# Where neighbouring blocks are paired in an S4 convolution: input spectra paired in DRAM by adding transfers, or kernel spectra paired by VectorE

## The chip, the cores and the metric

The kernel runs on one core of one Trainium2 chip. The metric is the device time of one execution in microseconds (us). The time before is the median of three runs.

## What is computed

Two layers, each of them an S4 convolution and a SwiGLU feed-forward, each on a normalised input and added to the stream `x` (2048 rows of 512):

```python
x = x + conv(layernorm(x));  x = x + ffn(layernorm(x))      # twice
# conv: K[d,l] = Re(sum_n C*exp(dt*A*l)*dt*B), y = causal convolution of u with K over 2048 rows, + u * Dskip
# ffn:  (silu(x @ w_gate) * (x @ w_up)) @ w_down,  w: 512 x 1376 and 1376 x 512
```

Both layers use the same convolution kernel `K` and the same weights.

## The kernel before

The convolution is done by blocks. The 2048 rows are four blocks of 512 rows (`NB = 4`). Each block of the input and of `K` is turned into a spectrum of odd frequencies (four groups `q` of 128 frequencies, two halves `h` of 256 columns, real and imaginary part: one tile of 128 x 512 f32, 256 KB). A block of the output, at these frequencies, is a sum of products of input spectra with kernel spectra; the part of a product that runs over a block's end belongs to the next block, with its real and imaginary part swapped and one of them negated. Before, this pairing of neighbours is put into the kernel spectra: what is stored as the spectrum of lag block k is that of block k plus the turned one of block k-1.

**Spectra of K (until some 345 us).** `K` is built in eight chunks of 64 columns. For each, VectorE and ScalarE make powers (`gen_e` L433-L440, `gen_g` L447-L475, `gen_turns`, `gen_trig`, `gen_exp`), TensorE multiplies them (`lags`, L485 and L486), the result goes through DRAM into the layout `kt` (`spread`, L498 and L500), and `spectra` multiplies it with DFT matrices (L515, products of 128x256 f32), two calls a chunk, each for two groups `q`. In `spectra` ScalarE copies the swapped and signed spectrum of block k-1 (L542) and the spectrum of lag block 0 (`w0r`, L543), VectorE adds the spectrum of block k (L545), and SP stores the sum to DRAM (`wdr`). For the last two chunks `first_parts` and `later_parts` (L576-L578) do this. The direct term `Dskip` is added inside the products by a matmul of one row (L517, L560). Beside this run the spectra of input blocks 0 and 1 of layer 0 (`direct`, L289-L293, stored by SP to `udr`), and the sizes of the FFN weights (`norms`, with the reduction L329 on VectorE).

The order of the three compute engines and of SP is written out by hand here: a list of (time, step) entries, sorted by time (`prepare`, `factors`, `use`, `second_block`, `weights`), with chunk starts 28 to 31 units apart. An engine takes its instructions in that order.

**The blocks (345 us on).** The order is `SEQ`: (layer, block) = (0,0), (0,1), (0,2), (1,0), (0,3), (1,1), (1,2), (1,3). While TensorE does the FFN of one entry (L886-L903), the convolution of the next entry goes on beside it. For each half and group: `forward` makes z on VectorE (L229), splits it for f16 (ScalarE L263, VectorE), TensorE multiplies (L273), ScalarE copies the spectrum `u` out (L275), and POOL stores it to `udr` for later blocks (L706, blocks 0 to 2 only). Then VectorE multiplies each input spectrum with its kernel spectrum (L754, 128x1024) and sums the products (L757): first lag block 0, `u` from SBUF with `w0r`, then k = 1 to b with `w` and `uu` that SP loads (L750, L752). L758 and L759 finish `y`, and TensorE (L773) and VectorE turn it back. Generators run one step ahead (`ahead`); beyond that the order of the engines in this part is set at build time by a scheduler with its own estimate of durations.

Of the kernel before, what the change touches and what calls it, by code (L numbers as in the profile page):

```python
# [11 lines left out]
F32 = mybir.dt.float32  # L12
# [10 lines left out]
P = 128  # L23
# [5 lines left out]
NL = 2  # L29
# [44 lines left out]
def kernel(ctx, tc, x, a_re, a_im, b_re, b_im, c_re, c_im, log_dt, d_skip,  # L74
# [65 lines left out]
    one = sb.tile([P, 1], F32, name="one")  # L140
    G.memset(one, 1.0)
# [4 lines left out]
    udr = [dram.tile([NB - 1, 2, 4, P, 2, HD], F32, name=f"udr{i}") for i in range(NL)]  # L146
# [95 lines left out]
    def forward(n, h, eh):  # L242
# [13 lines left out]
        for i, q in enumerate(QORD):  # L256
# [9 lines left out]
            with tc.high_priority(offset=BOOST):  # L266
# [8 lines left out]
                A.activation(u, pf, AF.Copy, scale=2.0 ** -16 if eh else 1.0)  # L275
            yield q, u
# [6 lines left out]
    def direct(b, h, q, n, space=psml):  # L283
# [9 lines left out]
        nc.sync.dma_start(udr[0][b, h, q], u)  # L293
# [194 lines left out]

    def spread_in(pk):
        ks = tl([P, 4, 16, 16], "ks", "nn")  # L490
        A.activation(ks, pk.rearrange("p d (c a) -> p a c d", a=4), AF.Copy)
        return ks
# [18 lines left out]
    def products(ch, pw, kt, k0, k1, q, order):  # L511

        for i, c in order:
            e = ek[q // 2][:, q % 2, c - 1, i] if c else ef[:, q, i]
            PE.matmul(pw[:, i], lhsT=e, rhs=kt[:, :, c + 4 * k0:4 * k1:4, :].rearrange("p g k d -> p k g d"), start=c == 0, stop=c == 3)  # L515
            if (i, c) == (0, 0) and k0 == 0:
                PE.matmul(pw[:, 0, 0], lhsT=one[0:1].to_broadcast([1, P]), rhs=dsk[:, ch * DC:(ch + 1) * DC], start=False, stop=False)  # L517

    def signs(q):

        return enumerate((-1.0, 1.0) if q % 2 == 0 else (1.0, -1.0))
# [4 lines left out]
    def spectra(ch, kt, q0):  # L526
# [4 lines left out]
        for j in range(2):  # L531
            products(ch, pw[:, j], kt, 0, NB, q0 + 2 * j, [(i, c) for i in range(2) for c in range(4)])
# [8 lines left out]
        for i, sign in signs(q0):  # L541
            A.activation(wv[:, :, i], pv[:, :, 1 - i, :3 * DC], AF.Copy, scale=sign)  # L542
        A.activation(w0r[:, h, q0::2, :, off:off + DC], wf[:, :, :, 0], AF.Copy)  # L543
        yield
        V.tensor_tensor(wv, pv[:, :, :, DC:], wv, OP.add)  # L545
# [5 lines left out]
    def first_parts(c0, q):  # L551
# [3 lines left out]
        for c in range(4):  # L555
            for i in range(2):
                e = ek[q // 2][:, q % 2, c - 1, i] if c else ef[:, q, i]
                PE.matmul(pw[:, i], lhsT=e, rhs=kt2[:, c0 + 2 - NCH:, :, c], start=c == 0, stop=c == 3)
                if (i, c) == (0, 0):
                    PE.matmul(pw[:, 0], lhsT=one[0:1].to_broadcast([1, P]), rhs=dsk[:, c0 * DC:], start=False, stop=False)  # L560
        A.activation(w0r[:, 1, q, :, off:], pw.rearrange("p i k g d -> p i (k g d)"), AF.Copy)

    def later_parts(ch, kt, qs=QORD):
# [3 lines left out]
        for q in qs:  # L567
            pw = psml([P, 2, NB - 1, 4, 16], "pw")
            products(ch, pw, kt, 1, NB, q, [(0, c) for c in range(4)])
            yield  # L570
            products(ch, pw, kt, 1, NB, q, [(1, c) for c in range(4)])
            yield
            w0 = w0r[:, h, q, :, off:off + DC].rearrange("p i (g d) -> p i g d", g=4)
            wo = next(slots)
            for i, sign in signs(q):
                A.activation(wo[:, i, 0], w0[:, 1 - i], AF.Copy, scale=sign)  # L576
                A.activation(wo[:, i, 1:], pw[:, 1 - i, :2], AF.Copy, scale=sign)
            V.tensor_tensor(wo, pw, wo, OP.add)  # L578
# [657 lines left out]
```

## Time and profile before

| | |
|---|---|
| runs (us) | 1185.04, 1185.14, 1187.83; median 1185.14 |
| profiled execution | 1186.51, its span 1184.7 |
| mean granted TensorE clock | 0.991 |
| TensorE busy | 1117.3 us (94%) |
| VectorE busy | 1006.2 us (85%) |
| ScalarE busy | 587.1 us (50%) |
| POOL busy | 92.2 us (8%) |
| DMA | 151.17 MB, 128 GB/s |

The page's rows carry the line of the kernel, the engine, the operation, out<-in, the shapes and the count; then the busy time and the mean duration of one in ns; then the idle time of the engine just before these instructions and what ended it. A row of a wait table is: engine, tile and line that waited, what was waited for, the time in all, how often, and the longest. A window row gives the busy time of each engine in a stretch of the span.

### The profile page before, as it was taken

The page shows a single profiled execution, that of the slowest core. Times are in us where ns is not written, and L with a number is a line of the kernel's source. Part 1 is how long each engine was busy: PE and PEld are TensorE (multiplying, and loading weights), DVE is VectorE, ACT ScalarE, POOL GpSimd, SP SyncE. Part 2 cuts the span into 40 slices and gives each one's busy share as a digit, 9 for nine tenths or more (in the row PEclk, how much of TensorE's full clock was granted, in tenths as well). Part 3 has the DMA queues.
Part 4 walks back from the last instruction along what each step waited for, and adds up shares of the span by engine and source line. Part 5 has one row for each costly group of instructions (what it writes and reads, how often), then busy time and mean ns, then how long its engine had stood idle before and what let it go on. Part 6 is the DMA issues. An engine that isn't in the chain of part 4 may idle for free.

```text
span 1184.7 us, 24523 instructions
## 1 busy us (share of the span) xinstructions
PE 1117.3 (94%) x10008; PEld 884.8 (75%) x10008; DVE 1006.2 (85%) x1591; ACT 587.1 (50%) x1180; POOL 92.2 (8%) x151
## 2 busy tenths in 40 slices
PE   1979999999789988999999999989999999999998
PEld 1868888888776857777778687858777686876875
DVE  7999999987789898999899999989994899983211
ACT  6677888833461554546654443655533452324211
POOL 1011111110000010002000000211000010000000
PEclk9989999999899999999999999999999999999999
DMA  6266666757484337432353354333544144312000
GB/s 231 91 162 149 162 166 162 182 179 240 125 271 140 115 119 200 118 96 84 92 152 128 112 165 155 96 104 115 149 116 165 46 121 130 118 49 45 14 24 18
DMA packets 136532, 151.17 MB, mean 128 GB/s; under 512 B 75474, under 2 KB 83666, under 8 KB 136419
## 3 DMA queue, kind: packets, MB, share of 16 engines
q1 hardware_dynamic: 129314, 126.47, 35.8%
q0 software_dynamic: 7104, 23.14, 7.3%
q8 instruction: 78, 1.28, 0.5%
q14 instruction: 36, 0.29, 0.1%
HBM read 101.85 MB, written 31.46 MB: 113 GB/s over the span
## 4 chain that ended last, share of the span: by engine, by line
PE 37%; DVE 27%; issue 4%; DMA 4%; ACT 2%; SPq 1%; POOL 0%; DVEq 0%; ACTq 0%; POOLq 0%
PE pgu L886 6%; PE pgu L887 6%; PE pgu L889 6%; DVE t L754 5%; DVE yk L757 5%; PE py L901 4%; PE py L902 3%; PE py L903 3%; PE pi L773 3%; PE pf L273 3%; DVE yk L754 2%; DVE z L229 2%; DVE sg L893 2%; DMA mix<-nn 1%; DVE bb L229 1%
## 5 line engine op out<-in xcount | busy, mean ns | idle before, releaser
L886 PE MATMUL pgu<-mix,wsl 128*128 128x256 f16 x1280 | 299.7, 273 | 6.9 <-DVE sg L893 4.4
L887 PE MATMUL pgu<-mix,wsl 128*128 128x256 f16 x1280 | 299.7, 273 | 0.0
L889 PE MATMUL pgu<-mix,wsl 128*128 128x256 f16 x1280 | 195.6, 273 | 0.0
L887 PEld LDWEIGHTS <-wsl 128*128 128x128 f16 x1280 | 125.5, 98 | 24.3 <-issue 8.0
L901 PE MATMUL py<-wsl,hh 128*128 128x512 f16 (+1 forms) x352 | 134.2, 381 | 8.6 <-DVE xg L906 6.9
L886 PEld LDWEIGHTS <-wsl 128*128 128x128 f16 x1280 | 125.4, 98 | 16.0
L889 PEld LDWEIGHTS <-wsl 128*128 128x128 f16 x1280 | 125.5, 98 | 14.9
L903 PE MATMUL py<-wsl,hl 128*128 128x512 f16 (+1 forms) x352 | 134.1, 381 | 0.2 <-DVE hl L895 0.2
L902 PE MATMUL py<-wsl,hh 128*128 128x512 f16 x320 | 121.8, 381 | 0.0
L754 DVE TENSOR_TENSOR t<-uu,w 128x1024 f32<-128x1024 f32 x96 | 116.9, 1218 | 2.6 <-DMA w<-wdr 2.4
L757 DVE TENSOR_TENSOR yk<-yk,t 128x1024 f32<-128x1024 f32 x96 | 116.9, 1217 | 0.3
L892 ACT ACTIVATE sg<-pgu,sc 128x512 f32<-128x512 f32 x80 | 54.6, 683 | 121.0 <-PE pgu L889 115.9
L893 DVE SCALAR_TENSOR_TENSOR sg<-pgu,sc,sg 128x512 f32<-128x512 f32 x80 | 59.6, 745 | 56.6 <-ACT sg L892 56.5
L515 PE MATMUL pw<-kt,ek 128*128 128x256 f32 (+1 forms) x384 | 94.1, 382 | 0.0
L894 ACT ACTIVATE hh<-sg 128x512 f16<-128x512 f32 x80 | 50.0, 626 | 76.1 <-DVE sg L893 76.0
L773 PE MATMUL pi<-yl,mix 128*128 128x256 f16 x576 | 78.9, 273 | 5.0 <-DVE yl L229 2.7
L515 PEld LDWEIGHTS pw<-kt,ek 128*128 128x128 f32 x384 | 70.8, 194 | 8.9
L273 PE MATMUL pf<-z,eh 128*128 128x256 f16 x576 | 74.9, 273 | 0.0
L754 DVE TENSOR_TENSOR yk<-u,w0r 128x1024 f32<-128x1024 f32 x56 | 68.2, 1218 | 1.5 <-ACT u L275 1.5
L902 PEld LDWEIGHTS <-hh 128*128 128x128 f16 (+1 forms) x352 | 34.6, 98 | 46.1 <-issue 10.6
L895 DVE TENSOR_TENSOR hl<-sg,hh 128x512 f16<-128x512 f32 x80 | 54.8, 686 | 15.6 <-ACT hh L894 15.5
L485 PE MATMUL pk<-re,g 128*32 128x64 f32 x1024 | 65.0, 317 | 2.8 <-DVE re L440 2.8
(239 smaller groups left out, 2154.3 us busy)
## 6 DMA issues: line engine op xcount, KB each, us to landing
w<-wdr SPq DMA_DIRECT2D x96, 256.0 KB, 2.7
uu<-udr SPq DMA_DIRECT2D x96, 256.0 KB, 3.0
udr<-u POOLq DMA_DIRECT2D x32, 256.0 KB, 2.7
g<-acc POOLq DMA_DIRECT2D x6, 1024.0 KB, 8.4
udr<-u SPq DMA_DIRECT2D x16, 256.0 KB, 2.1
n<-ndr SPq DMA_DIRECT2D x16, 256.0 KB, 3.9
n<-xdr SPq DMA_DIRECT2D x4, 1024.0 KB, 5.7
kdr<-ks SPq DMA_DIRECT2D x6, 512.0 KB, 2.7
```

The source lines that it names most:

```text
L273: PE.matmul(pf[:, o], lhsT=e, rhs=m, start=k == 0, stop=k == len(terms) - 1)
L515: PE.matmul(pw[:, i], lhsT=e, rhs=kt[:, :, c + 4 * k0:4 * k1:4, :].rearrange("p g k d -> p k g d"), start=c == 0, stop=c == 3)
L754: V.tensor_tensor(t, uu.unsqueeze(1).to_broadcast([P, 2, 2, HD]), w.unsqueeze(2).to_broadcast([P, 2, 2, HD]), OP.mult)
L757: V.tensor_tensor(yk, yk, t, OP.add)
L773: PE.matmul(pi[:, o], lhsT=e, rhs=m, start=k == 0, stop=k == len(terms) - 1)
L886: PE.matmul(o, lhsT=wgu(wi, k, 0)[:, fs], rhs=nh[:, k], start=k == 0, stop=False)
L887: PE.matmul(o, lhsT=wgu(wi, k, 1)[:, fs], rhs=nh[:, k], start=False, stop=False)
L889: PE.matmul(o, lhsT=wgu(wi, k, 0)[:, fs], rhs=nlo[:, k], start=False, stop=k == 3)
L893: V.scalar_tensor_tensor(sg, pgu[:, 1], sc6[:, 4:5], sg, OP.mult, OP.mult)
L901: PE.matmul(py[:, r], lhsT=hh[:n, f, rc], rhs=wd(f, 0)[:n], start=f == 0, stop=False)
L902: PE.matmul(py[:, r], lhsT=hh[:n, f, rc], rhs=wd(f, 1)[:n], start=False, stop=False)
L903: PE.matmul(py[:, r], lhsT=hl[:n, f, rc], rhs=wd(f, 0)[:n], start=False, stop=f == FT - 1)
```

## The change

- `udr` now holds **paired** input spectra: U_b plus the swapped, signed U_(b-1). For blocks 0 to 2, a new function `carry` makes a negated copy of one half of `u` on ScalarE (128x256) and issues two transfers of 128 KB to the next block's slot in `udr`, the halves swapped: from SP for the spectra made in the first part, from ScalarE's queue in `forward`. Then, for blocks 1 to 3, POOL stores `u` with an **adding transfer** into that slot (`accum_op=OP.add`). Block 3 has a slot now.
- The kernel spectra stay unpaired: L542's two copies, L545, L576, L577's two and L578 become one ScalarE copy.
- In the convolution, for b > 0, the spectrum for lag block 0 is loaded from `udr` too, so each step loads one `uu` more, and k runs from b down to 0.
- The direct term is added to lag 0 of `kt` by VectorE (`skip`, 64 elements in one partition, one call a chunk), in place of the one-row matmuls.
- In the list: the call of `skip` at t + 17.1, no fourth entry for `spectra`, the last part of `gen_e` in four entries, and two later times for the reductions of `weights`.

```diff
-    udr = [dram.tile([NB - 1, 2, 4, P, 2, HD], F32, name=f"udr{i}") for i in range(NL)]
+    udr = [dram.tile([NB, 2, 4, P, 2, HD], F32, name=f"udr{i}") for i in range(NL)]
...
 # forward
+            G.dma_start(udr[layer][b, h, q], u, **(dict(accum_op=OP.add) if b else {}))
+            if b < NB - 1:
+                carry(udr[layer][b + 1, h, q], q, u, nc.scalar)
             yield q, u
...
 # direct
-        nc.sync.dma_start(udr[0][b, h, q], u)
+        if b:
+            G.dma_start(udr[0][b, h, q], u, accum_op=OP.add)
+        else:
+            nc.sync.dma_start(udr[0][b, h, q], u)
+        carry(udr[0][b + 1, h, q], q, u, nc.sync)
...
+    def skip(ch, kt):
+        k = kt[0:1, :, 0]
+        V.tensor_tensor(k, k, dsk[:, ch * DC:(ch + 1) * DC].rearrange("p (g d) -> p g d", g=4), OP.add)
...
 # products
-            if (i, c) == (0, 0) and k0 == 0:
-                PE.matmul(pw[:, 0, 0], lhsT=one[0:1].to_broadcast([1, P]), rhs=dsk[:, ch * DC:(ch + 1) * DC], start=False, stop=False)
...
+    def carry(o, q, u, eng):
+        n = 1 - q % 2
+        t = tl([P, HD], "neg", "t1")
+        A.activation(t, u[:, n], AF.Copy, scale=-1.0)
+        eng.dma_start(o[:, 1 - n], t)
+        eng.dma_start(o[:, n], u[:, 1 - n])
...
 # spectra
-        for i, sign in signs(q0):
-            A.activation(wv[:, :, i], pv[:, :, 1 - i, :3 * DC], AF.Copy, scale=sign)
+        A.activation(wv, pv[:, :, :, DC:], AF.Copy)
         A.activation(w0r[:, h, q0::2, :, off:off + DC], wf[:, :, :, 0], AF.Copy)
-        yield
-        V.tensor_tensor(wv, pv[:, :, :, DC:], wv, OP.add)
...
 # later_parts
-            for i, sign in signs(q):
-                A.activation(wo[:, i, 0], w0[:, 1 - i], AF.Copy, scale=sign)
-                A.activation(wo[:, i, 1:], pw[:, 1 - i, :2], AF.Copy, scale=sign)
-            V.tensor_tensor(wo, pw, wo, OP.add)
+            A.activation(wo, pw, AF.Copy)
...
 # ssm_half
-            for k in range(b + 1):
-                if k == 0:
-                    w, uu = w0r[:, h, q], u
-                else:
+            for k in range(b, -1, -1):
+                w, uu = w0r[:, h, q], u
+                if k:
                     w = tl([P, 2, HD], "w", "w")
                     nc.sync.dma_start(w, wdr[k, h, q])
+                if b:
                     uu = tl([P, 2, HD], "uu", "uu")
                     nc.sync.dma_start(uu, udr[layer][b - k, h, q])
...
 # the list
-            at(t + 22.0, ge, 100)
+            for k in range(4):
+                at(t + 22.0 + 0.6 * k, ge, 1 if k < 3 else 100)
...
+            at(t + 17.1, lambda: skip(c, kt))
...
-            for k, t0, t1, t2, t3 in ((0, -1.4, 8.0, 13.9, 17.0), (1, 8.1, 14.5, 17.45, 19.5),
+            for k, t0, t1, t2, t3 in ((0, -1.4, 8.0, 13.9, 22.3), (1, 8.1, 14.5, 17.45, 22.9),
```

Lines of the changed kernel differ by a few from those of before. Two places show what moves on **VectorE**. The first is one chunk in the first part, from the last of `gen_turns` (`im<-im`) to the first rows of the next chunk's `gen_g`; `re` and `im` are the powers, `cmx` the reduction for the weight sizes, `spare` and `wo` the paired kernel spectra. Before:

```order
L386 ISA im<-im 128x2048
L329 TENSOR_REDUCE cmx<-nrm 128x1
L545 TENSOR_TENSOR spare<-pw,spare 128x768
L435 TENSOR_TENSOR re<-re 128x2048
L437 SCALAR_TENSOR_TENSOR im<-im,mu 128x1984
L440 TENSOR_TENSOR re<-re,mu 128x124x8 x2
L447 TENSOR_TENSOR xz<-xz,mz_158 128x960
L451 TENSOR_TENSOR g<-w_154,re 128x2x64
L452 TENSOR_TENSOR spare<-w_154,im 128x2x64
L433 TENSOR_TENSOR im<-im,re 128x2048
L545 TENSOR_TENSOR wo<-pw,wo 128x768
```

The same place of the changed kernel, where `kt_470<-kt_470,tdk` is `skip`:

```order
L391 ISA im<-im 128x2048
L497 TENSOR_TENSOR kt_470<-kt_470,tdk 1x4x16
L440 TENSOR_TENSOR re<-re 128x2048
L334 TENSOR_REDUCE cmx<-nrm 128x1
L442 SCALAR_TENSOR_TENSOR im<-im,mu 128x1984
L445 TENSOR_TENSOR re<-re,mu 128x124x8 x2
L452 TENSOR_TENSOR xz<-xz,mz_156 128x960
L456 TENSOR_TENSOR g<-w_152,re 128x2x64
L457 TENSOR_TENSOR spare<-w_152,im 128x2x64
L438 TENSOR_TENSOR im<-im,re 128x2048
```

Both additions of 768 elements are gone, `skip` stands where the first of them and the reduction stood, and the reduction follows one long instruction later.

The second place is the start of block (1,2) on VectorE. `z<-z` is the last step of the first group's spectrum on VectorE, before TensorE's L273; the product with `w0r` is the first that needs this spectrum. Before:

```order
L229 SCALAR_TENSOR_TENSOR z_3112<-z_3112 128x2x256
L229 SCALAR_TENSOR_TENSOR z_3112<-bt 128x256 x2
L229 SCALAR_TENSOR_TENSOR bb<-pi,sy,bb 128x512
L754 TENSOR_TENSOR yk<-u,w0r 128x1024
L229 SCALAR_TENSOR_TENSOR z_3112<-z_3112 128x2x256
```

In the changed kernel four more rows stand between `z<-z` and the first of these (an `sg`, two of `z<-bt`, an `hl`), and the product with `w0r` is the last:

```order
L227 SCALAR_TENSOR_TENSOR bb<-pi,sy,bb 128x512
L227 SCALAR_TENSOR_TENSOR z_3100<-z_3100 128x2x256
L227 SCALAR_TENSOR_TENSOR bb<-pi,sy,bb 128x512
L798 TENSOR_TENSOR bb<-bb 128x256
L227 SCALAR_TENSOR_TENSOR z_3100<-bt 128x256 x2
L788 TENSOR_TENSOR t_8777<-bb 128x256
L227 SCALAR_TENSOR_TENSOR t_8778<-bb 128x256
L227 SCALAR_TENSOR_TENSOR t_8786<-bb 128x256
L893 SCALAR_TENSOR_TENSOR sg_3099<-pgu,sc_92,sg_3099 128x512
L790 TENSOR_TENSOR xf<-xf,t_8777 128x256
L797 TENSOR_TENSOR bb<-bb 128x256
L754 TENSOR_TENSOR t<-uu,w0r 128x1024
```

The product that needs the newest spectrum has moved back behind work of the block before, and the second group's `z<-z` stands ahead of it.

33 lines of the change are left out of this document (12 added, 21 removed).

## The prediction

> **What bounds the kernel now.** I read the busy time of the engines in five stretches first: the start; the seven chunks from VectorE's first L440 to its last pair; the end of the first part; the blocks; the last FFN. The columns are stretch, its length, then TensorE, its weight loads, VectorE, ScalarE, POOL.
>
> ```profile
> 0.00:59.40 59.40, 33.24 (x136) 28.21 (x136) 49.62 (x95) 39.25 (x84) 5.43 (x23) 1.00 0.45 161
> 59.40:260.30 200.90, 194.94 (x2423) 163.96 (x2424) 193.06 (x225) 151.78 (x334) 30.94 (x58) 0.98 0.64 166
> 260.30:345.00 84.70, 75.50 (x697) 67.21 (x696) 65.65 (x120) 42.16 (x81) 2.30 (x2) 0.96 0.64 203
> 345.00:1065.00 720.00, 698.93 (x5844) 541.57 (x5842) 668.48 (x1110) 324.80 (x632) 51.76 (x64) 1.00 0.41 122
> 1065.00:1184.70 119.70, 114.74 (x914) 83.82 (x912) 29.43 (x45) 29.09 (x52) 1.80 (x4) 0.99 0.11 25
> ```
>
> In the second stretch TensorE is busy 97% and VectorE 96%: both are full, so a gain there needs both to lose work. In the fourth they have 97% and 93%. VectorE's waits in the second stretch, then those in the fourth that touch the convolution's products, show how little idle time there is to win or to hide in:
>
> ```profile
> DVE cmx L329 <- PE nrm L326: 2.8, 2, 1.6
> DVE spare L545 <- ACT w0r L543: 1.3, 1, 1.3
> DVE g L451 <- DMA g<-acc: 0.7, 1, 0.7
> ...
> DVE bb L229 <- PE pi L773: 6.9, 4, 3.5
> DVE t L754 <- DMA w<-wdr: 2.4, 2, 2.2
> DVE yk L754 <- ACT u L275: 1.5, 1, 1.5
> ```
>
> **The second stretch.** Rows of VectorE's additions and of an addition of 64 elements (the nearest to `skip`, though on 128 partitions), in this stretch alone:
>
> ```profile
> L545 DVE TENSOR_TENSOR wo<-pw,wo 128x768 f32<-128x768 f32 x6 | 5.8, 967 | 0.0
> L545 DVE TENSOR_TENSOR spare<-pw,spare 128x768 f32<-128x768 f32 x6 | 5.7, 952 | 1.3 <-ACT w0r L543 1.3
> L454 DVE TENSOR_TENSOR g<-g,spare 128x64 f32<-128x64 f32 x7 | 1.6, 225 | 0.0
> ```
>
> VectorE loses 5.8 + 5.7 = 11.5 us and gains seven calls of `skip`, 1.6 us: 193.06 - 11.5 + 1.6 = 183.2 us. For TensorE, three groups of products in a row, the middle one with the one-row matmul in it:
>
> ```profile
> 158.75 0.59 PE L515 MATMUL pw<-kt,ef 128*128 128x256 f32 x2
> ...
> 160.48 0.59 PE L515 MATMUL pw<-kt,ef 128*128 128x256 f32 x2
> ...
> 162.76 0.59 PE L515 MATMUL pw<-kt,ef 128*128 128x256 f32 x2
> ...
> L517 PE MATMUL pw<-tdk,one x52: 270/294/318, 80.0 to 261.8; 1*128 1x64 f32 x52
> ```
>
> Without it a group takes 160.48 - 158.75 = 1.73 us, with it 162.76 - 160.48 = 2.28: 0.55 us each. The 52 records are 26 calls (two passes each), of which 25 begin before 260.3: 13.8 us, and 194.94 - 13.8 = 181.1. Both engines fall, and by nearly the same. If VectorE keeps all its 7.8 us idle, the stretch takes 191.0 (-9.9); if the waits for the reduction and for L543 go (2.8 + 1.3: the first moves behind a long instruction, the second's instruction is gone), 186.9 (-14.0). By TensorE, with its 6.0 us idle kept, 187.1 (-13.8). The ends agree, so I take 13.5, less what `skip` costs as a wait.
>
> `skip` waits for `kt`, and VectorE's queue waits behind it. In one chunk the transfers of `kt`, the end of `gen_turns` and the first product with `kt` stand so:
>
> ```profile
> 160.35 1.78 SPq L500 DMA_DIRECT2D kt<-kdr  x4
> ...
> 164.25 2.74 DVE L386 CUSTOM_DVE_ANT_0 im<-im 128x256 uint16<-128x256 uint16 x4
> ...
> 168.67 0.59 PE L515 MATMUL pw<-kt,ef 128*128 128x256 f32 x2
> ...
> DMA to landing us min/median/max: 2.9/3.6/5.1
> ```
>
> The last transfer of four is issued some 161.7 and lands at 164.6 to 166.8. VectorE would reach `skip` at 166.99 less one L545, 166.0: it waits 0 to 0.8 us, 0 to 5.6 over seven chunks. TensorE wants `kt` at 168.67 less two one-row matmuls (1.1), 167.6, after `skip` is done. I take 1 us in all: **-12.5** (bounds -14 and -4.3, the last from 9.9 less 5.6).
>
> **The start** gains eight negated copies on ScalarE and sixteen transfers in SP's queue:
>
> ```profile
> L251 ACT ACTIVATE bt<-n x12: 400/404/419, 402.4 to 945.9; 128x256 f32<-128x256 f32 x12
> ...
> L500 SPq DMA_DIRECT2D kt<-kdr x24: 303/426/506, 72.9 to 220.6; - x24
> ```
>
> 8 x 0.40 = 3.2 us of ScalarE, which is busy 39.25 of 59.4, and 16 x 0.43 = 6.8 us of SP's queue, behind which later loads of `n1` wait. ScalarE's idle 20 us hides the first, the distance of those loads to their use the second. If neither did: +3.2. I take **+0.5**. Later, one copy a chunk (0.40) stands against L542's two becoming one: nothing. POOL's adding store there waits for `u` as SP's store did; behind it stand weight loads for the next chunk, and POOL is busy 30.94 of 200.9 us.
>
> **The end of the first part** loses one L545 (0.97), six of L578 and four one-row products:
>
> ```profile
> L578 DVE TENSOR_TENSOR wos<-pw,wos 128x384 f32<-128x384 f32 x4 | 2.2, 551 | 4.1 <-ACT wos L577 4.1
> ```
>
> At most 0.97 + 6 x 0.55 + 4 x 0.55 = 6.5 us, but neither engine is full there; I take **-1.5** (0 to -6.5).
>
> **The blocks.** Products and sums on VectorE stay as many. The spectrum for lag block 0 now goes through DRAM before its product. The start of block (1,2) in the trace, from the end of z to the product:
>
> ```profile
> 795.95 0.69 DVE L229 SCALAR_TENSOR_TENSOR z<-z 128x512 f16<-128x512 f32 x1 [0.69 <-ACT z L263]
> ...
> 798.08 1.36 PE L273 MATMUL pf<-z,eh 128*128 128x256 f16 x11
> ...
> 799.48 0.60 ACT L275 ACTIVATE u<-pf 128x512 f32<-128x512 f32 x1 [3.56 <-PE pf L273]
> ...
> 800.14 0.75 DVE L229 SCALAR_TENSOR_TENSOR bb<-pi,sy,bb 128x512 f32<-128x512 f32 x1 [2.69 <-PE pi L773]
> 800.37 0.60 POOL L706 DMA_DIRECT2D udr<-u  x1 [11.07 <-ACT u L275]
> 800.80 1.22 DVE L754 TENSOR_TENSOR yk<-u,w0r 128x1024 f32<-128x1024 f32 x1
> ```
>
> z ends at 796.64 and POOL issues at 800.37: 3.73 us. Then come the adding store and the load:
>
> ```profile
> uu<-udr SPq DMA_DIRECT2D x96, 256.0 KB, 3.0
> udr<-u POOLq DMA_DIRECT2D x32, 256.0 KB, 2.7
> g<-acc POOLq DMA_DIRECT2D x6, 1024.0 KB, 8.4
> n<-xdr SPq DMA_DIRECT2D x4, 1024.0 KB, 5.7
> ```
>
> No row has an adding store of 256 KB in DRAM. From below it is the plain one, 2.7; from above the adding one of 1024 KB into SBUF, 8.4. The latter is 8.4/5.7 = 1.5 times a plain load of its size, so I take about 1.3 times 2.7, 3.5. Chain: 3.73 + 3.5 + 3.0 = 10.2 us. Against it stands what VectorE does meanwhile. The sixteen rows from z to the product in the order, with durations of
>
> ```profile
> L229 DVE SCALAR_TENSOR_TENSOR z<-bt 128x256 f32<-128x256 f32 x96 | 36.5, 418 | 0.1
> L893 DVE SCALAR_TENSOR_TENSOR sg<-pgu,sc,sg 128x512 f32<-128x512 f32 x80 | 59.6, 745 | 56.6 <-ACT sg L892 56.5
> L895 DVE TENSOR_TENSOR hl<-sg,hh 128x512 f16<-128x512 f32 x80 | 54.8, 686 | 15.6 <-ACT hh L894 15.5
> ```
>
> are ten of 128x256 (4.2), four of 0.745 (3.0) and two of 0.69 (1.4): 8.6 us. So VectorE waits some 1.7 us, where before it waited 2.69 in this place. By the same sum the starts of (0,2), (0,3) and (1,3) have 11.7, 7.7 and 8.4 us of work, and those of before only 3.7, 2.9 and 2.9 against a chain of 4.2 to the product. Waits: 0 + 2.5 + 1.7 + 1.8 = 6.0 after, 0.5 + 1.3 + 2.7 + 1.3 = 5.8 before: nothing changes. Inside the blocks most groups have 14 to 40 us of work in between, as the spectra are now made two steps ahead; the shortest are two groups of (1,1) with 11.2 and 11.7, still over 10.2. Behind a late load in SP's queue wait the next `w` and `uu` and the transposes for the FFN.
>
> ScalarE gains 32 copies and 64 issues in this stretch: 32 x 0.40 + 64 x 0.43 = 40 us, in 395 that it has idle. They stand in front of its work on `sg` and `hh`, on which VectorE and TensorE's matmul groups hang. Hidden wholly they cost 0, a third exposed 13; I take **+2**.
>
> **Sum**: 0.5 - 12.5 - 1.5 + 2 = -11.5 us. The profiled execution is 1.4 us over the median; 1186.5 - 11.5 = 1175.0 there, and against the median 1185.1 - 11.5, so I forecast **1173.6 us**.
>
> **Rivals.**
>
> *The adding store lands late, and the kernel is slower.* With a landing of L the chain is 6.7 + L. At L = 6.4 the four starts wait 1.4 + 5.4 + 4.5 + 4.7 and the two groups of (1,1) 1.9 + 1.4: 19.3, less 5.8 of before, which eats the 13.5 us that the other terms give without ScalarE's. That is the point from which it decides. At L = 7.1, the longest plain store of before, it is 23.5 - 5.8 = 17.7, and 1185.1 - 13.5 + 2 + 17.7 = 1191. For it: the 1024 KB row. Against it, POOL's stores amid a nearly full VectorE:
>
> ```profile
> L706 POOL DMA_DIRECT2D udr<-u x32: 539/542/607, 410.9 to 886.4; - x32
> ...
> DMA to landing us min/median/max: 2.3/2.7/7.1
> ```
>
> The issue never takes over 0.61 us, and half land within 2.7. The Trainium skill ("SBUF — State Buffer", section "SBUF: two separate sides") speaks against adding transfers here: they are issued from GpSimd, whose descriptor writing is locked out while VectorE runs a two-port instruction, so that 0.62 us become 3.1. By that page L would be about 6.0 as an estimate, and the kernel some 1185; the issue times above show no such lock with this VectorE work. Chance 0.16.
>
> *ScalarE becomes the bound in the blocks.* A third of its 40 us exposed: 1185.1 - 13.5 + 13 = 1185, no change. For it: sg and hh are taken in order behind the issues; against it: 45% busy. Chance 0.09.
>
> *The work goes, and the time stays in the first part.* `skip` ties VectorE to the landing of `kt`, and TensorE to `skip`; 5.6 us of waits and no idle time won: -4.3 in place of -12.5, 1182. Chance 0.10.
>
> *The idle time of the blocks' starts goes too.* The products of older blocks can now run before the newest spectrum, and fill the 5.8 us: 1168 or less. Chance 0.10.
>
> **Numbers.** The forecast (1168 to 1180) has 0.55. Times within 0.3% (3.6 us, about what a measurement of this kernel can tell from no change) are 1181.6 to 1188.7: the second and third rival mostly, 0.16. Faster holds the forecast, the last rival and a part of the third, 0.70; slower, the late store, 0.14. The range, 1162 to 1190, takes in all but the outer parts of the first and last rivals.
>
> **What would show it.** Right: the chunk's pitch on VectorE (200.9/7 = 28.7 us) at 26.5 to 27.0, no wait of the reduction, `skip` with under 1 us idle before it; landing of the adding stores under 4 us; products with `w0r` that wait at block starts for about 2 us each; ScalarE some 40 us busier in its queue without longer waits of VectorE for sg. Wrong: a second stretch over 192 us, or waits for `uu` in every step.

## The result, and the profile after

The changed kernel takes **1222.74 us** (median of 4 runs, 1220.03 to 1225.59) against 1186.34 us of before (4 runs): ratio **1.0307**, 95% interval 1.0273 to 1.0340. It is slower by 36 us, where 11.5 us faster was forecast. The profiled execution has a span of 1223.7 us.

The windows of the changed kernel, in the columns of the prediction's first table; the blocks' window ends 39 us later than before's, so that both hold the same work:

```profile
59.40:260.30 200.90, 182.75 (x2382) 158.78 (x2383) 186.06 (x221) 156.11 (x339) 37.43 (x65) 0.96 0.72 178
345.00:1104.00 759.00, 707.04 (x5833) 542.84 (x5832) 671.90 (x1111) 333.06 (x668) 66.16 (x81) 0.99 0.56 147
1104.00:1223.70 119.70, 114.72 (x915) 83.86 (x912) 28.92 (x43) 27.17 (x48) 1.10 (x3) 1.00 0.09 25
```

In the first window the work fell nearly as forecast: VectorE from 193.06 to 186.06, TensorE from 194.94 to 182.75 (the window here also holds some 3 us of what comes next). The time did not. Both engines, busy 96 and 97% before, now have 15 and 18 us of idle time there. In the blocks the work is nearly the same and lasts 39 us longer (759 against 720).

VectorE's waits in the first window, all of them:

```profile
DVE g L456 <- DMA g<-acc: 8.8, 3, 4.7
DVE kt L497 <- ACT kt L519: 1.2, 1, 1.2
DVE g L456 <- ACT re L405: 0.9, 1, 0.9
DVE cmx L334 <- PE nrm L331: 0.3, 1, 0.3
```

The reduction's wait went (2.8 to 0.3), `skip` waits 1.2 us, as forecast; TensorE waits 2.9 us for `skip` once, where none was forecast. But the wait for the 1 MB adding transfer into the generating factors g, 0.7 before, is 8.8 us, and TensorE waits 7.3 more for it. The rows of VectorE and POOL in one chunk (start, duration, engine, line), first of the changed kernel, then of the kernel before:

```profile
132.83 2.29 DVE L469 TENSOR_TENSOR acc<-g,xz 128x2048 f32<-128x2048 f32 x1
...
138.40 0.20 DVE L497 TENSOR_TENSOR kt<-kt,tdk 1x64 f32<-1x64 f32 x1
...
139.52 1.60 POOL L322 DMA_DIRECT2D st<-in_B_w_gate_dram  x3 [6.50 <-ACT sq L328]
...
141.10 1.27 POOL L470 DMA_DIRECT2D g<-acc  x1
...
145.08 1.14 DVE L452 TENSOR_TENSOR xz<-xz,mz 128x960 f32<-128x960 f32 x1
...
150.94 0.29 DVE L456 TENSOR_TENSOR g<-w,re 128x128 f32<-128x128 f32 x1 [4.73 <-DMA g<-acc]
```

```profile
133.29 2.29 DVE L464 TENSOR_TENSOR acc<-g,xz 128x2048 f32<-128x2048 f32 x1
...
137.59 1.60 POOL L317 DMA_DIRECT2D st<-in_B_w_gate_dram  x3 [6.58 <-ACT sq L323]
139.17 1.27 POOL L465 DMA_DIRECT2D g<-acc  x1
...
147.34 0.28 DVE L451 TENSOR_TENSOR g<-w,re 128x128 f32<-128x128 f32 x1
```

In both kernels three weight loads stand ahead of the transfer in POOL's queue and wait for ScalarE's squares. Before, the transfer was issued 3.6 us after `acc` was ready (135.58), and VectorE took g 8.2 us after the issue without a wait. In the changed kernel `acc` is ready at 135.12 and the transfer is issued 6.0 us later, since ScalarE's squares come 1.9 us later than before (138.73 against 136.79); g is there 9.8 us after the issue. VectorE would have come to L456 at 146.21, 11.1 us after `acc` against 11.8 before: the addition that went, less `skip`, took only some 0.7 us from the cover of this wait of 4.7. The rest is that VectorE reaches its wait early while ScalarE's squares, and with them the issue, are late, and that the transfer lands later.

The end of the first part has a second new wait, at the last chunk's `skip`, with ready work queued behind it:

```profile
265.27 0.42 DVE L759 TENSOR_TENSOR yf<-yk 128x256 f32<-128x256 f32 x1
275.54 0.21 DVE L497 TENSOR_TENSOR kt<-kt,tdk 1x64 f32<-1x64 f32 x1 [9.85 <-ACT kt L519]
275.69 1.21 DVE L754 TENSOR_TENSOR yk<-mix,w0r 128x1024 f32<-128x1024 f32 x1
```

In the blocks (345 to 1105), VectorE's four longest waits, and the longest of SyncE's queue:

```profile
DVE t L754 <- DMA uu<-udr: 23.5, 14, 2.7
DVE hl L895 <- ACT hh L894: 13.1, 7, 6.0
DVE bb L227 <- PE pi L773: 12.7, 5, 3.1
DVE nn L839 <- DMA mix<-nn: 10.0, 6, 4.6
...
SPq L752 <- DMA udr<-u: 133.7, 26, 19.4
```

The first, for a loaded spectrum, did not exist before; ten of its 14 waits, 19.3 us, stand at products with `w0r`, which take the newest spectrum. The other three were 6.2, 6.9 and 2.9 us before. The rows of POOL's stores, 40 adding ones and the eight plain ones of block (1,0) (duration in ns: shortest, median, longest; then the landing):

```profile
L274 POOL DMA_DIRECT2D udr<-u x48: 539/861/922, 415.3 to 1069.7; - x48
...
DMA to landing us min/median/max: 2.3/4.6/8.4
```

### The profile page after: what moved, and what is told of

The parts are those of the page before. It is cut to its first block, busy times and chain, and to the rows that moved or that the text cites. A ratio compares the mean times of both kernels' runs of the same rounds, so it can differ in the third digit from the quotient of the medians.

```text
span 1223.7 us, 24686 instructions
## 1 busy us (share of the span) xinstructions
PE 1111.3 (91%) x9948; PEld 878.6 (72%) x9948; DVE 995.9 (81%) x1580; ACT 597.8 (49%) x1197; POOL 113.6 (9%) x174
## 4 chain that ended last, share of the span: by engine, by line
PE 24%; DVE 21%; DMA 13%; issue 11%; ACT 3%; SPq 2%; POOL 1%; DVEq 0%; ACTq 0%; POOLq 0%
PE pgu L886 5%; PE pgu L887 4%; PE pgu L889 4%; DMA uu<-udr 4%; DVE t L754 3%; DMA mix<-nn 3%; DVE yk L757 3%; DMA udr<-u 3%; DVE yk L754 2%; PE py L901 2%; PE py L903 2%; PE py L902 2%; DVE z L227 2%; PE pi L773 2%; DMA w<-wdr 2%
## 5 line engine op out<-in xcount | busy, mean ns | idle before, releaser
L773 PE MATMUL pi<-yl,mix 128*128 128x256 f16 x576 | 79.4, 274 | 13.8 <-ACT yl L762 8.5
L525 PE MATMUL pw<-kt,ek 128*128 128x256 f32 (+1 forms) x384 | 91.3, 374 | 0.0
L271 PE MATMUL pf<-z,eh 128*128 128x256 f16 x576 | 77.5, 281 | 1.1 <-DVE z L227 0.9
L274 POOL DMA_DIRECT2D udr<-u x48 | 39.4, 821 | 387.1 <-ACT u L273 318.2
L754 DVE TENSOR_TENSOR t<-uu,w0r 128x1024 f32<-128x1024 f32 x48 | 58.8, 1224 | 19.5 <-DMA uu<-udr 19.3
L490 PE MATMUL pk<-re,g 128*32 128x64 f32 x1024 | 62.5, 301 | 11.4 <-DMA g<-acc 7.3
L271 PEld LDWEIGHTS <-eh 128*128 128x128 f16 x576 | 57.8, 100 | 19.6 <-issue 10.3
```

The lines of the kernel that those rows point to most:

```text
L271: PE.matmul(pf[:, o], lhsT=e, rhs=m, start=k == 0, stop=k == len(terms) - 1)
L490: PE.matmul(o, lhsT=g[:, 0, :, d], rhs=re[:, 0:64, d], start=True, stop=False, tile_position=(0, 32 * grp))
L754: V.tensor_tensor(t, uu.unsqueeze(1).to_broadcast([P, 2, 2, HD]), w.unsqueeze(2).to_broadcast([P, 2, 2, HD]), OP.mult)
L773: PE.matmul(pi[:, o], lhsT=e, rhs=m, start=k == 0, stop=k == len(terms) - 1)
```

## The experiments

Seventeen kernels ran. Each ratio is to the kernel before, measured beside it. Three theories of the blocks were on record: the **trip** of the newest spectrum through DRAM with SyncE's queue behind it; **ScalarE's** carry; the **adding transfers**.

The order of the blocks is set by a scheduler, and most edits change it. By the rows of VectorE, e2c has the changed kernel's order in the blocks, e10 that of e3, e9 that of e5 and e14 that of before. Every other comparison of blocks below also compares two orders.

### The blocks: trip and carry, alone and together

**e1_old_slot**: `udr[layer][b - k, ...]` becomes `udr[layer][b - max(k, 1), ...]`.

> What it is: the changed kernel with one index altered. The product of lag 0 loads the slot of the block before instead of the newest slot (the output then uses the wrong spectrum at lag 0), so every load, copy and adding transfer stays and only the wait of the newest load for its own adding store is gone. Trip theory (the blocks lose their 39 us because the newest spectrum goes out to DRAM and back, and because SyncE's queue, issued in order, stands still behind that load): the wait of 133.7 us on SyncE's queue for that store goes, VectorE's 23.5 us of waiting for loaded spectra falls below 8, and the kernel takes 1185 to 1195 us. ScalarE theory (the 80 extra copies and 160 extra issues of the carry in the blocks are late for the work behind them): nothing that it blames has changed, 1215 to 1225. Transfer theory (27 MB more traffic and slower adding stores hold up every other transfer): 1215 to 1225 as well. The order of instructions in the blocks shifts somewhat with the altered dependency, which may be worth a few us either way.

Measured: 1202.35 us, ratio 1.0137 (1.0120 to 1.0154). 20 us of 36 come back, in another order of the blocks: the trip seems to matter, but it isn't all. (The copies and issues that the expectation counts as 80 and 160 are 32 and 64 in the trace.)

**e2c_plain_store**: the order on all five engines is that of the changed kernel, so that only the transfer differs. The store then overwrites the carried half, so the pairing is left out in these blocks.

```diff
-            G.dma_start(udr[layer][b, h, q], u, **(dict(accum_op=OP.add) if b else {}))
+            G.dma_start(udr[layer][b, h, q], u)
```

> What it is: the changed kernel with GpSimd's store of a block's spectrum plain instead of adding (the carried half is overwritten, so in blocks formed after the first part the pairing is left out). The order on every engine is that of the changed kernel; copies, issues, and the load of the newest spectrum stay. It prices the adding itself: in the profiles, 0.9 against 0.54 us of issue and about 4.6 against 2.7 us to landing. Trip theory: the trip is shorter by some 2.3 us for each of the loads that wait for it; of the 48 stores about a dozen end on the path, so 10 to 25 us of the 39 come back: 1198 to 1213. ScalarE theory: the copies and their issues are all there, within 4 us of the changed kernel: 1218 to 1226. Transfer theory: the bytes are the same but the slower read-and-write at the target is gone, 1200 to 1215, with the loads of kernel spectra (3.5 us to landing) back near the 2.7 of before.

Measured: 1202.98 us, ratio 1.0141 (1.0111 to 1.0171). Its waits, VectorE's for the loaded spectra and SyncE's for the store, and its store's row:

```profile
DVE t L754 <- DMA uu<-udr: 6.2, 5, 2.2
```

```profile
SPq L752 <- DMA udr<-u: 103.4, 20, 17.5
```

```profile
L274 POOL DMA_DIRECT2D udr<-u x48: 539/542/622, 418.1 to 1047.2; - x48
...
DMA to landing us min/median/max: 2.3/3.1/6.6
```

A store that is 0.32 us shorter to issue and 1.5 us shorter to land takes 23.5 us of VectorE's waits down to 6.2 and gives back 20 us, with ScalarE's carry still there. SyncE's queue still stands 103 us for the store, of 134, so that standing by itself is not the price. ScalarE's theory falls with this run.

**e2_no_carry**: the plain store, and `carry` in `forward` left out.

> What it is: as the run with the plain store, and the carry is left out of the blocks too (no negated copies, no transfers from ScalarE's queue; the pairing is left out in those blocks). What stays of the change in the blocks is the load of the newest spectrum from DRAM. Against the run with the plain store it prices ScalarE's extra copies and issues. Trip theory: the round trip of 2.7 + 3 us and SyncE's queue behind it stay; 3 to 8 us better than with the carry, 1193 to 1208, still above the kernel before. ScalarE theory: everything that it blames is gone, 1180 to 1188. Transfer theory: 20 MB less traffic, 1183 to 1192.

Measured: 1199.75 us, ratio 1.0120 (1.0088 to 1.0152). Against e2c the intervals overlap: copies and issues on ScalarE cost 2.5 us by the ratios, or nothing that can be told.

**e6_old_slot_no_carry**: e2_no_carry with the index of e1.

> What it is: the run without the carry (plain store, no pairing in the blocks), with lag 0 also loading the slot of the block before, so that it waits for no store of its own block (the output uses a wrong spectrum at lag 0). It completes a square: trip and carry with its adding store both (the changed kernel, blocks 842 us from the first addition of L906 to the last), no trip (820), no carry and no adding (816), now neither. The kernel before has 801. If trip and carry make the loss between them, this run has 801 to 806 us there and takes 1183 to 1189 us. If a third thing in the change does (the extra 256 KB load for each group, or the lags taken from the oldest to the newest), 812 or more stays, and it takes 1194 or more.

Measured: 1198.46 us, ratio 1.0083 (1.0057 to 1.0109). The square, in parts of before's time: both 3.07%, no trip 1.37%, no carry and adding 1.20%, neither 0.83%. So the trip alone costs 0.37% and the carry with its adding alone 0.54%, some 11 us as a sum (for the trip alone the intervals overlap); together they cost 2.24%, **27 us**. A rest stays. Against the runs with lag 0 in SBUF (e3, e7, e10, e13 below, 1.0006 to 1.0046) it is 0.4 to 0.8%, 4 to 9 us. By the blocks alone, from the first to the last of VectorE's additions of the FFN's result to `x`, it is more. Their rows in before, the changed kernel, e6 and e3 (shortest, median and longest in ns, then the first and the last start in us):

```profile
L906 DVE SCALAR_TENSOR_TENSOR xg<-py,sc,xg x24: 737/746/752, 379.5 to 1180.6; 128x512 f32<-128x512 f32 x24
L906 DVE SCALAR_TENSOR_TENSOR xg<-py,sc,xg x24: 742/750/769, 377.4 to 1219.6; 128x512 f32<-128x512 f32 x24
L904 DVE SCALAR_TENSOR_TENSOR xg<-py,sc,xg x24: 732/744/751, 381.1 to 1196.4; 128x512 f32<-128x512 f32 x24
L906 DVE SCALAR_TENSOR_TENSOR xg<-py,sc,xg x24: 736/743/751, 385.1 to 1187.2; 128x512 f32<-128x512 f32 x24
```

That is 801, 842, 815 and 802 us; e1 has 820, e2c 818 and e2_no_carry 816, and e7, e10 and e13 have 801 to 802. These are single profiles. By them the blocks lose 41 us, of which trip and carry together are 27 and the rest 13 to 14. What stands ahead of the blocks is no longer in the changed kernel than before (377 against 379.5), though it is in e3 (385): with the same order of the first part, that time differs by several us from run to run.

**e8_newest_load_gpsimd**: `(nc.sync if k else G).dma_start(uu, ...)`.

> What it is: the changed kernel, whole, with the load of the newest spectrum issued on GpSimd's queue, behind the store that it waits for, instead of on SyncE's. The trip is as long as before, but nothing stands behind it on SyncE: next loads of spectra, and the transposes into mix. If the standing queue makes the trip dear, the waits for mix (ScalarE 33 us, VectorE 10) go back to the 13 and 3 of before, and the kernel takes 1200 to 1212. If it is the trip's own length, VectorE waits for uu as long as it did (23.5 us) and the time stays at 1217 to 1225. If the load on GpSimd's queue lands later than on SyncE's, it gets worse than 1225.

Measured: 1229.78 us, ratio 1.0334 (1.0294 to 1.0374), no better than the changed kernel. VectorE's wait, and what the moved load waited for on POOL:

```profile
DVE t L754 <- DMA uu<-udr: 28.1, 16, 4.3
```

```profile
POOL uu L752 <- DVE t L754: 114.8, 14, 11.8
```

The order of the blocks differs as well. The wait for the store left SyncE, and GpSimd's queue now stands for a free buffer `uu`, with the next adding stores behind it. The part of my theory that blamed SyncE's standing queue isn't borne out.

**e12_add_in_sbuf**: the carry is brought into the new spectrum in SBUF by an adding transfer, lag 0 reads SBUF, and the store is plain. ScalarE makes two copies for a carry in place of one, and `skip` of the last chunk stands as in e5 below.

```diff
-            G.dma_start(udr[layer][b, h, q], u, **(dict(accum_op=OP.add) if b else {}))
...
+            if b:
+                G.dma_start(u, udr[layer][b, h, q], accum_op=OP.add)
+            if b < NB - 1:
+                G.dma_start(udr[layer][b, h, q], u)
```

> What it is: the whole computation, with the later addition of the last chunk's direct term, and the pairing of the blocks turned round: the block before leaves its carry in the next slot as in the changed kernel (two copies and two transfers from ScalarE's queue), and an adding transfer brings it from DRAM into the new spectrum in SBUF, where lag 0 reads it; a plain store for the later blocks follows. The adding is the same work, but there is one transfer between ScalarE's copy and VectorE's product instead of two, no extra load, and nothing stands behind it on SyncE's queue. If the loss of the blocks is the adding store with the load behind it (27 us) and the extra load (14 us), the blocks take 803 to 812 us and the kernel 1184 to 1194. If adding traffic or the carry on ScalarE's queue is dear wherever it lands, it takes 1200 to 1215.

Measured: 1209.65 us, ratio 1.0183 (1.0146 to 1.0220), 16 us above what I expected and in the range of the other theory, by which adding and carry are dear wherever they land. One transfer in place of two in the trip was worth less than I thought:

```profile
DVE t L761 <- DMA u<-udr: 19.1, 8, 5.7
```

```profile
POOL udr L282 <- DMA u<-udr: 68.2, 20, 6.0
```

VectorE waits nearly as long, and the plain store holds POOL's queue until the addition has landed. Against e5, which shares its first part, it loses 2.3%, 27 us. So pairing by adding transfers is dear in SBUF too; how much of that is the carry's, this run doesn't separate.

### The rest of the blocks

**e7_lags_reversed** (the changed first part with before's blocks, k from b down to 0), **e10_two_buffers** (the same first part and blocks, `uu=2`), and **e13_unused_load** (e7 with the extra load into a buffer that nothing reads):

> What it is: the run with the changed first part and the blocks of before (spectrum of lag 0 from SBUF, plain store, no pairing there), with one thing taken over from the changed blocks: the products run from the largest lag to lag 0. The square of runs left 14 us of the blocks' loss when neither the trip nor the carry was there. If the order of the lags makes these 14 us, the blocks take 812 to 818 us here instead of 802, and the kernel 1200 or more. If the extra load for each group does (one more 256 KB transfer, one more turn of the three buffers uu), the blocks stay at 800 to 805 and the kernel within 4 us of 1192.85.

> What it is: the same run with two buffers uu instead of three, and nothing else. In the changed blocks 144 loads a run turn over three buffers, where 96 did: on average each has two thirds of the time between its issue and its use. Two buffers for 96 loads give the same two thirds. If the turnover makes the 14 us, the blocks take 810 us or more and the kernel 1200 to 1207. If it is the load's own traffic or its issue on SyncE's queue, the time stays within 4 us of 1192.85.

> What it is: the run with the lags reversed and the blocks of before (blocks 802 us, no pairing there), to which each group adds the changed kernel's extra transfer: 256 KB from the slot of the block before into a buffer uu, on SyncE's queue, which nothing reads. If the extra load costs by its traffic, its issue and its turn of the buffers, the blocks take 811 us or more and the kernel some 10 us over the run without it (1190.3), 1198 or more. If it costs only because VectorE's product of lag 0 has to wait for it, the blocks stay within 4 us of 802 and the kernel at 1187 to 1194.

Measured: 1190.34 us, 1.0024 (1.0006 to 1.0042); 1194.24 us, 1.0041 (1.0021 to 1.0060); 1188.39 us, 1.0006 (0.9988 to 1.0024). None costs anything beside e3's 1.0046. The order of the lags, the buffers' turnover and the load's traffic are out, as far as runs with lag 0 in SBUF can show it.

**e17_old_slot_ahead** and **e18_newest_ahead**: lag 0's spectrum is loaded in `forward`.

```diff
-                u = tl([P, 2, HD], "u", "u")
+                u = tl([P, 2, HD], "u", "uu" if b else "u")
...
+            if b:
+                u = tl([P, 2, HD], "un", "u")
+                nc.sync.dma_start(u, udr[layer][b - 1, h, q])
```

> What it is: the run with neither trip nor carry (lag 0 loads the slot of the block before, blocks 815 us), with that load issued where the spectrum is formed, one group ahead of its use and into the two buffers u, instead of at its use into the three buffers uu (the fresh spectrum takes a buffer uu until its store has landed). Same transfers, same bytes (wrong spectrum at lag 0, no pairing in the blocks). If the 14 us come from the place at which the load is issued, the blocks take 800 to 806 us and the kernel 1184 to 1191. If any dependence of lag 0 on a load costs them, 812 or more stays and the kernel takes 1195 or more.

> What it is: the changed kernel, whole, with the load of the newest spectrum issued where the spectrum is formed, right behind its adding store, into the two buffers u. The trip is the same 4.7 + 3 us, and SyncE's queue still stands behind the load until the store has landed, but the product comes a group later than that. If the place of the issue makes 14 us of the loss and part of the trip's 27, the kernel takes 1195 to 1210. If the queue that stands behind the load makes the trip dear, the waits of SyncE's queue for that store stay over 100 us and the kernel stays above 1215.

Measured: 1324.10 us, 1.1128 (1.1104 to 1.1152), and 1370.30 us, 1.1500 (1.1474 to 1.1525). My edit made another coupling, so the runs settle nothing. Fresh spectra now take turns with the lags' loads in the three buffers `uu`, and the engines wait for each other around the products; in e17:

```profile
PE pi L774 <- ACT yl L763: 51.1, 11, 18.0
```

By elimination the rest (4 to 9 us by the ratios, 13 to 14 by the profiles) is left to VectorE's depending on a load at lag 0, or to the order that the scheduler chooses for it. The second stands untested; against it speaks only that the blocks with lag 0 in SBUF took 800 to 804 us in several orders.

### The first part

**e3_first_part**: the changed first part, before's blocks.

> What it is: the changed first part (spectra of the kernel not paired on VectorE, direct term added to lag 0 of the kernel) with the blocks of the kernel before: lag 0 takes the spectrum from SBUF, the store is plain, no carry in the blocks (which leaves out the pairing there). It prices the first part alone. By the traces the first part gave only 2 us, since what VectorE and TensorE no longer do was taken up by waits for the 1 MB adding transfer into the generating factors: I expect 1181 to 1186 us, with 7 to 10 us of VectorE's time before the product of L456 and about as much of TensorE's spent on that transfer, as in the changed kernel. If instead what I forecast for the first part held (14 us) and the blocks ate part of it, it takes 1170 to 1174. If the moves in the schedule of the blocks, rather than the trip, made the 39 us, it stays above 1200.

Measured: 1192.85 us, ratio 1.0046 (1.0029 to 1.0062). The first part alone doesn't gain, it **loses** 5 us.

**e5_skip_later**: e3, and for the last chunk

```diff
-        skip(c, kts[1])
         take(conv[0], 1)
         scales()
         split(1, 0)
+        skip(c, kts[1])
```

> What it is: the run with the changed first part and the blocks of before (no pairing in the blocks), in which the last chunk's addition of the direct term stands behind the next product and the weights' scales in VectorE's order, right ahead of the products that need it. In the run without this move VectorE stood 9.6 us at that addition (269.2 to 278.8) with ready work behind it, and the weights' scales came 9 us later than before. If this wait is what made that run 6.8 us slower than before, 5 to 8 us come back: 1185 to 1188. If the first part is bound elsewhere there (ScalarE's kt, the clock), it stays at 1190 to 1194.

Measured: 1183.64 us, ratio 0.9953 (0.9935 to 0.9972). Against e3 that is 0.93%, **11 us**, from one instruction's place in VectorE's order: the wait of 9.6 us at `skip` (6.1 in this run) had held up the weights' scales. The blocks of the two runs are equally long (802 and 801 us), so what is won lies ahead of them.

**e5b_transfer_first**: e5, with POOL in the order of the program and the second group of weight loads behind the 1 MB transfer (8.1 becomes 11.3 in the list).

> What it is: the run with the later addition, and GpSimd's instructions of the first part held to the order of the program with the second group of weight loads 3.2 us later there, which puts the 1 MB adding transfer into the generating factors ahead of the loads that wait for ScalarE's squares; the order of the blocks hardly changes. If the wait for that transfer (VectorE 8.8 us and TensorE 7.3 us in the changed kernel) took what the first part should have gained, the last chunk starts 5 to 9 us earlier than without it, and the kernel takes 1177 to 1182. If the first part is bound by the tie between the engines through the addition to lag 0, it gains 2 us or less.

Measured: 1231.36 us, ratio 1.0353 (1.0313 to 1.0393), a plain miss. The wait for that transfer is gone from VectorE's list, but these came, and the weight loads' landing changed:

```profile
PE nrm L330 <- ACT sq L327: 47.0, 8, 13.2
```

```profile
st<-in_B_w_gate_dram POOLq DMA_DIRECT2D x16, 172.0 KB, 7.9
```

```profile
151.34 1.26 POOL L469 DMA_DIRECT2D g<-acc  x1 [7.20 <-DVE acc L468]
152.09 2.19 POOL L321 DMA_DIRECT2D st<-in_B_w_gate_dram  x3
...
160.77 1.51 ACT L327 ACTIVATE sq<-st 128x344 bf16<-128x344 f32 x3 [7.82 <-DMA st<-in_B_w_gate_dram]
```

The weight loads now land in 7.9 us (3.8 in e5), and those behind the transfer are issued late as well: the transfer waits for `acc`, and they wait behind it. In the chunk shown the squares come to their place 0.9 us after the loads' issue and wait 7.82 us for them; in e5 the last loads ahead of the squares at this place of a chunk were issued 7.4 us before these (130.66 and 138.02), and the squares didn't wait. The squares stand at the head of ScalarE's order, and TensorE's sums stand behind them. So the run priced this new tie, and not the transfer's start.

**e9_squares_earlier**: e5, and in the list `(0, -1.4, 8.0, ...)` becomes `(0, -1.4, 6.5, ...)`.

> What it is: the run with the later addition of the last chunk's direct term (1183.6 us), with ScalarE's squares of the first group of weight loads ahead of its copy of the lags in each chunk instead of behind it. There ScalarE stood idle waiting for TensorE's lags (38 us in that run) with the squares behind; the next weight loads wait on GpSimd's queue for these squares, and the 1 MB adding transfer stands behind those loads. VectorE's order is the same, word for word. If the transfer's late start took the first part's gain, VectorE's 5.8 us and TensorE's 7.8 us of waiting for it fall below 3, and the kernel takes 1174 to 1181. If the transfer is late by its own 8.6 us of landing, or the time goes to the next wait (TensorE for re, the products for the addition to lag 0), it stays at 1181 to 1186.

Measured: 1178.29 us, ratio 0.9918 (0.9894 to 0.9943). The waits for the transfer, VectorE's and TensorE's, which were 5.8 and 7.8 us in e5:

```profile
DVE g L455 <- DMA g<-acc: 4.7, 2, 3.3
```

```profile
PE pk L489 <- DMA g<-acc: 2.7, 3, 1.7
```

By the ratios this is 4 us faster than e5, and the two intervals just overlap. VectorE's wait fell less than I expected, and its wait for the reduction rose from 0.3 to 4.1 us; most of what fell is TensorE's. So the transfer's late start took some 4 us of the first part's gain, as far as these runs can tell.

**e14_before_squares** (before, with the squares earlier) and **e15_direct_term** (before with the direct term added by `skip`, in the later place, and the squares earlier; the whole computation, paired by VectorE):

> What it is: the kernel before, with the squares of the first group of weight loads ahead of the copy of the lags on ScalarE in each chunk (one number of the plan), and nothing of the change. VectorE's, TensorE's and SyncE's orders are the same as in the kernel before. In the kernel before the adding transfer's wait was nearly covered (0.7 us on VectorE), by the work that the change took away; so if the first part of before is bound by VectorE's and TensorE's own work, this gives 0 to 2 us: 1185 to 1188. If the transfer's start bounded before as well, it gains 4 to 6 us like the corrected first part of the change: 1182 to 1184.

> What it is: the kernel before with one half of the change, whole in its computation: the direct term is added to lag 0 by VectorE (for the last chunk in the later place) and its 4-byte products on TensorE go, while VectorE goes on pairing the kernel spectra and the blocks are those of before; with the squares ahead as in the run above. The run without VectorE's pairing took 1178.3 us; the pairing is 13 additions of 0.95 us. If the first part is bound by the sum of VectorE's work, these come back and it takes 1183 to 1190, so that the direct term alone is worth 0 to 4 us. If the gain of that run came from the direct term and the transfer's start, it takes 1177 to 1183 and beats both kernels with the full computation.

Measured: 1185.50 us, 0.9986 (0.9971 to 1.0002), no difference that can be told; and **1178.84 us, 0.9932 (0.9911 to 0.9953)**, the fastest that computes everything, faster than both kernels. TensorE's, its weight loads' and VectorE's busy time from 59.4 to 250, of before and of e15:

```profile
59.40:250.00 190.60, 184.65 (x2351) 156.32 (x2352) 184.12 (x218) 147.05 (x324) 29.34 (x55) 0.98 0.66 168
```

```profile
59.40:250.00 190.60, 175.95 (x2353) 153.30 (x2354) 187.46 (x226) 148.44 (x325) 29.60 (x56) 0.96 0.63 168
```

TensorE has lost its one-row products, and VectorE runs at 98% where it had 97%. Without the pairing, e9 is 0.14% faster than e15, and the intervals overlap: taking 11.5 us of additions from VectorE, with the carry that the first part gets for it, was worth about 2 us at most.

## Why the prediction was wrong, step by step

- **The second stretch (-12.5)** failed. The work fell by 7 us on VectorE and 12 on TensorE, against 9.9 and 13.8 forecast, but the step that VectorE and TensorE keep their idle time was wrong: it rose from 7.8 to 15 and from 6.0 to 18 us. The g<-acc wait, quoted at 0.7 us, became 8.8. The transfer had just fitted: its issue hangs on ScalarE's squares, which did not come earlier when VectorE did. From VectorE's first L445 (59.62) to the last chunk's (257.40) the stretch takes 197.8 us, over the 192 that were to show the forecast wrong. Before's last L440 starts at 260.25, so 2.9 us were won in this profile; in the other runs with the same first part that row starts between 255.4 and 262.0, so the gain can't be told from nothing. With transfer and `skip` mended the stretch gives more, but by e15 against e14 it is the direct term's move that gives it, some 6 us (with the last `skip` in its later place); the pairing's 11.5 us were hardly on the path.
- **`skip` (1 us)** was right inside the stretch for VectorE (1.2); that TensorE would not wait for it was not (2.9). For the last chunk, in "the end of the first part (-1.5)", it was not priced at all: 11 us by e3 and e5. There `kt` comes from TensorE and ScalarE, late, and the weights' scales were queued behind it.
- **The start (+0.5)** held: 41.33 against 41.13 at VectorE's first powers of a chunk.
- **The blocks (+2)** failed, and by the profiles this is the whole loss. Two steps failed. The landing of the adding store, "about 1.3 times 2.7, 3.5", is 4.6 at the median and up to 8.4: 1.5 times the plain store at the same place, which takes 3.1. By the prediction's own sum L = 4.6 would cost only some 3.5 us, so the larger fault is the cover, "most groups have 14 to 40 us of work in between": products with `w0r` waited ten times, where four block starts were priced, each wait some 2 us (0.5 to 2.7). So the rival was right in direction, but its deciding point, L = 6.4, was too high. The count of work was taken from VectorE's order; it left out what the newest load meets on SyncE's queue, where its line waits 133.7 us for stores and 74.2 for a free buffer in the changed kernel. Which of these stands on the path was not shown. e2c prices the adding in that place at 20 us.
- **Trip and carry** were costed as a sum; by the square they are not one: 11 us apart, 27 together. Its four runs have different orders in the blocks, so a part of that may be the order's.
- **ScalarE (40 us hidden)** was right: e2c keeps all of it (34 us by the changed kernel's rows) and e2_no_carry drops it, with 2.5 us between, inside the intervals. The rival that made ScalarE the bound fell.
- **The Trainium skill** ("SBUF — State Buffer", section "SBUF: two separate sides") was cited for a lock that would delay GpSimd's issue while VectorE runs, with L about 6.0 as an estimate and 1185 us. The trace does not show it: the adding issue takes 0.86 us at the median and never over 0.93, the plain one 0.54 in the same order of work. So what it takes more goes with the adding form, and no issue here is near 3.1.

The account by the ratios: first part alone 0.46% (in e3), lag 0 from a load 0.37% (e6 over e3), trip and carry together 2.24%, in all 3.07%. Of this, 1.66% is shown with nothing but the transfer changed (e2c); the rest is read from runs with other orders.

## What to carry to other kernels

A wait of 0.7 us in a trace can belong to a transfer that just fits: before work is taken off a full engine, look for the transfers that land under it, and for the other engines on which their issue hangs, which don't get faster with it. A value that takes a new way through DRAM is priced with the queue and the buffers ahead of its load, in each place where it is used, and two delays in one chain are not priced apart. An addition that waits for another engine belongs in the order right ahead of its user, behind all work that is ready.

## What the runs showed of the hardware

An adding transfer of 256 KB into DRAM takes 0.86 to 0.93 us of GpSimd to issue and lands 4.6 us later, against 0.54 and 3.1 for the plain one at the same place of the same order; from DRAM into SBUF it lands in 4.6 too (e12). Weight loads of 172 KB that are issued on GpSimd's queue right behind an adding transfer, of 256 KB or 1 MB, land in 7.9 us (e5b), against 3.8 in e5's order.

In these three runs the granted TensorE clock was lower where TensorE was busy less. From 59.4 to 250 it was 0.98 with 184.65 us busy (before), 0.96 with 175.95 (e15), and in e5b:

```profile
59.40:250.00 190.60, 147.64 (x1940) 125.59 (x1941) 144.85 (x178) 128.56 (x281) 27.98 (x49) 0.88 0.59 142
```

In e14 it was 0.97 with 186.41, so the order isn't strict, and which causes which isn't settled by these runs.
